# The last of the 24 sets of four weight-block sums, on VectorE in place of GpSimd

## The chip, the cores and the metric

The kernel runs on one core of one Trainium2 chip. Its time is the device time of one launch in microseconds (us); what counts is the median of several runs. The core has five engines with queues of their own: TensorE (PE in the rows), VectorE (DVE), ScalarE (ACT), GpSimd (POOL) and SyncE (SP), which here starts nearly all DMA transfers. Each queue is worked in its order, so an instruction that waits holds up everything behind it on the same engine.

## The reference

Attention over a sliding window of 64 tokens (4 batches, 8 heads, 576 tokens, 64 numbers a head), then two layers of the same form on 2304 tokens:

```
x = attention(q, k, v)                      # 2304 x 512
h = x @ w_in1;  g = h - tanh(h);            x = g @ w_out1      # 512 -> 2048 -> 512
h = x @ w_in2;  g = h * sigmoid(1.702 * h); x = g @ w_out2      # 512 -> 2048 -> 512
```

The four weight matrices arrive as 64-bit floats; the kernel makes 32-bit ones of them by bit operations on the chip.

## The kernel before, in words

**Precision.** Every operand of a large product is split into a high part (`hi`, `gh`, written by ScalarE) and the rest (`lo`, `gl`, a subtraction on VectorE), and `three` (line 783) takes three matmuls for one: high by high, high by low, low by high. So each step on TensorE needs a high part from ScalarE and then a low part from VectorE.

**Seven products for eight.** Layer 1's output product for its last two blocks of 512 tokens, and layer 2 for two units of 1024 tokens, are multiplied by Winograd's form of Strassen's method: seven block products P1 to P7, with sums and differences of blocks on both sides. On the weight side each of the 16 weight slabs, taken in pairs, gives four sums S1 to S4 (`wd_sums`, lines 394 to 400): S1 = A21 + A22, S2 = S1 - A11, S3 = A11 - A21, S4 = A12 - S2, each on 128 x 256 numbers. There are three matrices to prepare (m = 0 is layer 2's w_in, m = 1 its w_out, m = 2 layer 1's w_out) and eight pairs j of each, 24 sets in all, all on GpSimd. For m = 0 (`plan_wd`, lines 463 to 487) a pair of slabs is loaded into `raw`, ScalarE and VectorE convert it into two `cw` tiles (`conv_abs`, `conv_mant`, `conv_low`, `conv_sign`), the sums are written over the `raw` tile, and four stores by SyncE (line 433) put the two `cw` tiles and the two halves of `raw` into a DRAM tensor `wd0` to `wd7`; layer 2 reads it later (line 517). The last set made is (j, m) = (7, 0).

**The stage around the change.** While the last weights are prepared, TensorE ends layer 1's hidden products (`psh`) and begins layer 1's output products for the last two blocks (`ob`): seven products of eight steps, 56 steps, a step being six matmuls (`o_prod`, line 1064). A step's operand is a tile `ug`; for P6, P7 and P4 VectorE first forms it by a subtraction (`u_sub`, line 1040), then ScalarE writes `gh` (line 1049) and VectorE `gl` (line 1053), through three buffers of each. The weights of four steps come by one 1 MB load (`load_w1`, line 1029), 14 loads in all into three buffers: load number n can start when the steps on load n-3 are done. In the same stretch SyncE starts loads for layer 2's first unit (`xt`, line 957, and `x2b`, line 961, which VectorE adds to `xt` at line 965); an `x2b` takes one of four small buffers that its addition frees. After the 56 steps comes layer 2's first block of 256 tokens (`psh` and `acc`), and then the two units.

**What sets the order.** The class `Plan` plays the whole program through once, with an estimated length for each task and a priority from its due time; the order in which it comes to the tasks is then fixed, engine by engine. So a task's engine and estimated length can move other tasks in the order, also on other engines.

Of the kernel before, what the change touches and what calls it, by code (L numbers as in the profile page):

```python
# [24 lines left out]
class Plan:  # L25
# [11 lines left out]
    def add(self, engs, fn, prio, after=(), acq=(), rel=(), size=0, behind=None):  # L37


        t = dict(engs=engs, fn=fn, prio=prio, acq=acq, rel=rel, size=size, n=len(self.tasks), outs=[], next=[], left=0, at=None, own={})  # L40
        for a in after:
            if a is not None:
                a["outs"].append(t)
                t["left"] += 1
        if behind is not None:
            behind["next"].append(t)
            t["left"] += 1
        self.tasks.append(t)
        return t
# [126 lines left out]
def attn_moe2_kernel(  # L176
# [20 lines left out]
    nc = tc.nc  # L197
# [3 lines left out]
    _, NG, NP, _ = q.shape  # L201
# [14 lines left out]
    NJ = KF // 2  # L216
# [33 lines left out]
    add = plan.add  # L250
# [44 lines left out]
    def first(*key):  # L295
        return min(due["h", s] for s in steps if s[0][: len(key)] == key)
# [89 lines left out]
    def pair_of(j, m, i):  # L386
        layer = 1 if m == 2 else 2
        if i < 2:
            return bits[layer, 2 * j + i, m].bitcast(F32)
        return raw[layer, 2 * j, m].bitcast(F32).rearrange("p a b -> p (a b)")[:, (i - 2) * NB : (i - 1) * NB]  # L390

    PAIRS = (((A11, A12), (A21, A22), (S1, S2), (S3, S4)), ((A11, A21), (A12, A22), (S1, S2), (S3, S4)), ((A11, A21), (A12, A22), (S1, S2), (S3, S4)))

    def wd_sums(j, m):
        x = {}
        for i in range(4):
            p = pair_of(j, m, i)
            x[PAIRS[m][i][0]], x[PAIRS[m][i][1]] = p[:, :HB], p[:, HB:]
        for o, a, b, op in ((S1, A21, A22, ALU.add), (S2, S1, A11, ALU.subtract), (S3, A11, A21, ALU.subtract), (S4, A12, S2, ALU.subtract)):
            nc.gpsimd.tensor_tensor(out=x[o], in0=x[a], in1=x[b], op=op)  # L400

    def wd_hi(j, m, i):
        o = stage[j, i, 0] = st.tile([P, NB], F32R, tag="s", name="wds")
        nc.scalar.activation(o, pair_of(j, m, i), AF.Copy)
# [16 lines left out]
    def rebuild(j, i):  # L421
        if i == 0:
            raw[1, 2 * j, 2] = cv.tile([P, NB, 2], U32, tag="raw", name="raw")
        x = bits[1, 2 * j + i, 2] = st.tile([P, NB], F32, tag="cw", name="cw", bufs=K["cw"])
        hi, lo = halves((1, 2 * j + i, 1))
        nc.vector.tensor_tensor(out=x, in0=hi.bitcast(F32), in1=lo.bitcast(F32), op=ALU.add)
# [11 lines left out]
    def plan_s(j, d, near, last):  # L438
        c = [converted[1, 2 * j + i, 1] for i in range(2)]
        a = [add({"DVE": 0.62}, lambda _: rebuild(j, 0), d, c + near + last, acq=("raw", "cw", "cw"))]  # L440
        a.append(add({"DVE": 0.62}, lambda _: rebuild(j, 1), d + 1, a))
        sums = add({"POOL": 2.8}, lambda _: wd_sums(j, 2), d + 3, a)
        add({"none": 0.0}, lambda _: None, d, [sums], rel=[("cw", a[0]), ("cw", a[0])])
        sts, lows = [], []
        for i in (2, 3):
            h = add({"ACT": 0.54}, lambda _, i=i: wd_hi(j, 2, i), d + 2 * i, [sums], acq=("s", "wds"))
            lo = add({"DVE": 0.62}, lambda _, i=i: wd_lo(j, 2, i), d + 2 * i, [h])
            for b, w in enumerate((h, lo)):
                sts.append(add({"SP": 0.6}, lambda _, i=i, b=b: wd_store(j, 2, i, b), d + 2 * i, [w], size=P * NB * 4))
            add({"none": 0.0}, lambda _: None, d, [sts[-2], lo], rel=[("s", h), ("wds", h)])  # L450
            lows.append(sts[-1])
        add({"none": 0.0}, lambda _: None, d, lows, rel=[("raw", a[0])])
        wd_done[2, j] = sts
        for i in range(2):
            a_done.setdefault(2 * j + i, []).append(a[i])
        return [sums]
# [6 lines left out]
    def plan_wd(j, m, d, after):  # L463
        signs, ls, cs = [], [], []
        both = add({"SP": 1.2}, lambda _: [load_w((2, 2 * j + i, m)) for i in (1, 0)], d - 5, after, acq=("raw", "raw"), size=2 * P * NB * 8)
        for i in range(2):
            key = (2, 2 * j + 1 - i, m)

            def go(e, fn, t, *a, key=key, **kw):
                return add({e: t}, lambda _: fn(key), d + 3 * i, *a, **kw)  # L470

            l = both
            c = absol = go("ACT", conv_abs, 0.55, [l] + cs, acq=() if i else ("cw", "cw"))
            for fn, x in ((conv_mant, 0.34), (conv_low, 0.6)):
                c = go("DVE", fn, x, [c])
            signs.append(go("DVE", conv_sign, 0.6, [c], rel=[] if i else [("raw", l)]))
            ls.append(l)
            cs.append(absol)
        sums = add({"POOL": 2.8}, lambda _: wd_sums(j, m), d + 6, signs)
        los, sts = [], []  # L480
        if m == 0:
            for i in range(4):
                sts.append(add({"SP": 0.6}, lambda _, i=i: wd_store(j, 0, i), d + 6 + 2 * i, signs[1 - i :][:1] if i < 2 else [sums], size=P * NB * 4))
            wd_done[m, j] = sts
            add({"none": 0.0}, lambda _: None, d, sts[:2] + [sums], rel=[("cw", cs[0]), ("cw", cs[0])])
            add({"none": 0.0}, lambda _: None, d, sts[2:], rel=[("raw", ls[0])])
            return both
        for i in range(4):
            h = add({"ACT": 0.54}, lambda _, i=i: wd_hi(j, 1, i), d + 6 + 2 * i, signs[1 - i :][:1] if i < 2 else [sums], acq=("s", "wds") + (("s", "wds") if i < 2 else ()))
            los.append(add({"DVE": 0.62}, lambda _, i=i: wd_lo(j, 1, i), d + 6 + 2 * i, [h]))  # L490
            for b, w in enumerate((h, los[-1])):
                sts.append(add({"SP": 0.6}, lambda _, i=i, b=b: wd_store(j, 1, i, b), d + 6 + 2 * i, [w], rel=[("s", h), ("wds", h)] if b and i < 2 else [], size=P * NB * 4))
            add({"none": 0.0}, lambda _: None, d, sts[-2:-1] + los[-1:], rel=[("s", h), ("wds", h)])
        wd_done[m, j] = sts
        add({"none": 0.0}, lambda _: None, d, los[:2] + [sums], rel=[("cw", cs[0]), ("cw", cs[0])])
        add({"none": 0.0}, lambda _: None, d, [sts[5], sts[7]], rel=[("raw", ls[0])])
        return both
# [631 lines left out]
    for t, m in masks.items():  # L1129
        nc.gpsimd.memset(m, 0.0)  # L1130
        for kind, r in zip(t, (slice(0, W), slice(W, P))):
# [5 lines left out]
            for base, cm, step, op in conds:  # L1137
                nc.gpsimd.affine_select(
                    out=m[r], in_=m[r], pattern=[[step, P]], base=base,
# [8 lines left out]
    for i in range(NEARLY):  # L1148
        a = 2 * i
# [14 lines left out]
    for i in range(8):  # L1164
        z = turns[0 if i < 2 else 1 if i < 4 else 2]
        d = first(*z) - K["ahead"][i]
# [3 lines left out]
    for bi in range(2, NB1):  # L1170
        t0, n = blocks[1][bi]
        d = first(1, bi)
# [4 lines left out]
    for f in range(KF):  # L1177
        for i in range(2):
            d = due["hp"[i], next(s for s in steps if s[1] == f)]
# [278 lines left out]
    for what, s, *rest in seq:  # L1458
        if what == "O":
            if (0, 0) not in wd_done:  # L1460
                last = None
                for n in range(2 * NJ):
                    d = K["wd"][0] + K["wd"][1] * n
# [156 lines left out]
    for o in order:  # L1620
        d = due[o]
# [50 lines left out]
```

## Time and profile before

| | |
|---|---|
| median of 3 runs | 856.62 us (855.27 to 856.74) |
| profiled execution | 854.67 us |
| its span, first to last instruction | 852.9 us |
| mean granted TensorE clock | 0.992 |
| TensorE, VectorE, ScalarE, GpSimd busy | 822.5, 679.1, 469.8, 213.9 us |
| DMA, mean over the span | 218 GB/s |

The profile is of one execution. Times in its rows are us from the span's start. A busy time counts the engine's own instructions; a granted clock of 1.00 is the full one (2.4 GHz), 0.50 the lower level (1.2 GHz). A row of waits says which engine and line waited for which other, how long in all, how many times, and how long at most. In a row of the order in time, the bracket at the end is the idle time before the instruction and what ended it.

### The profile page before, as it was taken

To read this page: it belongs to the slowest core of one execution; us is meant where nothing else is said; L and a number is where in the kernel's file an instruction comes from. 1 tells how busy PE (TensorE), PEld (TensorE's weight loads), DVE (VectorE), ACT (ScalarE), POOL (GpSimd) and SP (SyncE) were. 2 spreads that over 40 slices of the span, in tenths; PEclk is the share of its full clock that TensorE was granted. 3 is DMA by queue.
4 is the path that set the end of the run, shared out by engine and by line. 5 is a ranking of instruction groups with operands and counts; after the bars stand their busy time and mean duration, and the time that the engine had idled before them with its cause. 6 is when DMAs were issued, how large, how long until landed. Compare 5 with 4: busy or idle time off the path is not lost.

```text
span 852.9 us, 15375 instructions
## 1 busy us (share of the span) xinstructions
PE 822.5 (96%) x5639; PEld 715.5 (84%) x5639; DVE 679.1 (80%) x1085; ACT 469.8 (55%) x1040; POOL 213.9 (25%) x211
## 2 busy tenths in 40 slices
PE   7898999999999999999859999999999999999998
PEld 5787888888899988887748888888899998889998
DVE  6999998879899878757939885577899867778954
ACT  7887566457677656334416654344545544444443
POOL 3110001531422213253910000366500006662000
PEclk9999999999999999999969999999999999999999
DMA  9785977788897976696367998321666742226572
GB/s 329 269 283 169 277 247 263 265 283 269 272 287 268 295 243 207 224 296 209 119 219 242 324 336 278 112 87 38 215 230 219 246 161 87 80 73 246 178 225 71
DMA packets 115163, 186.34 MB, mean 218 GB/s; under 512 B 7440, under 2 KB 81168, under 8 KB 115088
## 3 DMA queue, kind: packets, MB, share of 16 engines
q1 hardware_dynamic: 114656, 184.84, 65.5%
q8 instruction: 44, 0.72, 0.4%
q10 hardware_dynamic: 432, 0.52, 0.2%
q14 instruction: 31, 0.25, 0.1%
HBM read 131.86 MB, written 53.48 MB: 217 GB/s over the span
## 4 chain that ended last, share of the span: by engine, by line
PE 77%; DVE 9%; DMA 4%; POOL 3%; ACT 3%; issue 2%; SPq 1%; DVEq 0%; ACTq 0%; POOLq 0%
PE ob L783 23%; PE psh L783 22%; PE m L783 17%; PE acc L783 12%; POOL raw L400 3%; PE psa L701 1%; PE psa L718 1%; DMA x2b<-xs 1%; PE psa L645 1%; DMA wo<-wdo 1%; DVE gl L1053 1%; ACT s L677 1%; DVE cw L337 1%; DVE s L694 1%; DMA w<-wdo 1%
## 5 line engine op out<-in xcount | busy, mean ns | idle before, releaser
L783 PE MATMUL psh<-xh,w 128*128 128x512 f32 (+1 forms) x672 | 194.7, 362 | 0.0
L1049 ACT ACTIVATE gh<-ug 128x512 fp32r<-128x512 f32 x168 | 105.2, 629 | 110.3 <-PE ob L783 96.5
L783 PE MATMUL ob<-ws,gh 128*128 128x256 f32 x896 | 162.0, 283 | 0.0
L1053 DVE TENSOR_TENSOR gl<-ug,gh 128x512 fp32r<-128x512 f32 x168 | 120.6, 721 | 42.8 <-ACT gh L1049 40.3
L783 PEld LDWEIGHTS ob<-ws,gh 128*128 128x128 f32 x896 | 140.0, 192 | 0.2
L783 PEld LDWEIGHTS psh<-xh,w 128*128 128x128 f32 x672 | 121.6, 189 | 20.2 <-issue 1.0
L1037 POOL TENSOR_TENSOR ug<-ug,g 128x512 f32<-128x512 f32 x48 | 68.2, 1428 | 256.2 <-ACT g L1033 255.9
L783 PE MATMUL ob<-ws,gl 128*128 128x256 f32 x448 | 126.9, 283 | 1.7 <-DVE gl L1053 1.7
L783 PE MATMUL psh<-xl,w 128*128 128x512 f32 (+1 forms) x336 | 120.9, 360 | 1.6 <-DVE xl L738 1.6
L400 POOL TENSOR_TENSOR raw<-cw 128x256 f32<-128x256 f32 x48 | 59.3, 1236 | 240.8 <-DVE cw L343 84.6
L783 PE MATMUL acc<-gh,w 128*128 128x512 f32 (+1 forms) x416 | 113.4, 344 | 0.0
L783 PE MATMUL m<-xu,ws 128*128 128x512 f32 x384 | 92.3, 389 | 0.0
L783 PEld LDWEIGHTS ob<-ws,gl 128*128 128x128 f32 x448 | 86.0, 192 | 2.0 <-DVE gl L1053 1.9
L783 PEld LDWEIGHTS m<-xu,ws 128*128 128x128 f32 x384 | 71.9, 188 | 14.9
L783 PE MATMUL ob<-gh,w 128*128 128x512 f32 x224 | 71.6, 398 | 12.4 <-DMA w<-wdo 12.3
L783 PEld LDWEIGHTS acc<-gh,w 128*128 128x128 f32 x416 | 73.6, 189 | 9.9 <-issue 0.9
L1011 DVE TENSOR_TENSOR ug<-ug,m 128x512 f32<-128x512 f32 x80 | 54.8, 685 | 31.2 <-PE m L783 30.0
L783 PEld LDWEIGHTS psh<-xl,w 128*128 128x128 f32 x336 | 63.5, 189 | 11.1 <-DVE xl L738 2.2
L783 PE MATMUL acc<-gl,w 128*128 128x512 f32 (+1 forms) x208 | 70.8, 340 | 0.0
L526 DVE TENSOR_TENSOR ws<-wr,ws 128x1024 fp32r<-128x1024 f32 (+1 forms) x40 | 53.6, 1343 | 10.3 <-ACT ws L521 10.0
L783 PEld LDWEIGHTS ob<-gh,w 128*128 128x128 f32 x224 | 43.0, 192 | 22.2 <-issue 12.7
L521 ACT ACTIVATE ws<-wr 128x1024 fp32r<-128x1024 f32 (+1 forms) x40 | 38.7, 969 | 41.4 <-PE m L783 33.0
(119 smaller groups left out, 1471.0 us busy)
## 6 DMA issues: line engine op xcount, KB each, us to landing
ws<-wdo SPq DMA_DIRECT2D x28, 1024.0 KB, 5.3
raw<-in_w_in SPq DMA_DIRECT2D x32, 512.0 KB, 5.5
raw<-in_w_out SPq DMA_DIRECT2D x32, 512.0 KB, 4.7
w<-wdo SPq DMA_DIRECT2D x14, 1024.0 KB, 6.5
wdo<-wds SPq DMA_DIRECT2D x48, 256.0 KB, 3.2
wr<-wd SPq DMA_DIRECT2D x24, 512.0 KB, 6.3
wdo<-w SPq DMA_DIRECT2D x32, 256.0 KB, 4.8
wdo<-raw SPq DMA_DIRECT2D x32, 256.0 KB, 3.4
```

What stands on the lines that cost most here:

```text
L337: nc.vector.scalar_tensor_tensor(out=bits[key], in0=raw[key][:, :, 0], scalar=29, in1=bits[key], op0=ALU.logical_shift_right, op1=ALU.bitw ...
L400: nc.gpsimd.tensor_tensor(out=x[o], in0=x[a], in1=x[b], op=op)
L521: nc.scalar.activation(new_ws(key)[:, 0, : x.shape[1]], x, AF.Copy)
L526: nc.vector.tensor_tensor(out=t[:, 1], in0=x, in1=t[:, 0].bitcast(F32), op=ALU.subtract)
L645: nc.tensor.matmul(ps[h][part(j, h), p, :], lhsT=qt[j][r, p, :], rhs=kt[j][r, :, p, :], start=not on_pe, stop=not on_pe or p == NP - 1,)
L677: nc.scalar.activation(s[:, h, p, :], x[:, p, :], AF.Exp, bias=nm[:, h, p : p + 1], scale=scale, accum_out=sm[:, h, p : p + 1],)
L694: nc.vector.tensor_tensor(out=s[:, h], in0=s[:, h], in1=sm[:, h].unsqueeze(2).to_broadcast([P, NP, P]), op=ALU.mult)
L783: nc.tensor.matmul(ps, lhsT=a, rhs=b, start=first and i == 0, stop=last and i == 2, skip_group_check=onto)
L1011: nc.vector.tensor_tensor(out=u_val(u, j, o), in0=u_val(u, j, a), in1=mb[u, j, n], op=ALU.add)
L1037: eng.tensor_tensor(out=u_val(u, j, o), in0=u_sum(u, j, o), in1=ut[u, j, o, "g"], op=ALU.mult)
L1049: nc.scalar.activation(gh, u_val(u, j, PROD[n][1]), AF.Copy)
L1053: nc.vector.tensor_tensor(out=gl, in0=u_val(u, j, PROD[n][1]), in1=gh.bitcast(F32), op=ALU.subtract)
```

## The change

The set (7, 0) is planned for VectorE with an estimated length of 1.6 us, where all sets were planned for GpSimd with 2.8 us; `wd_sums` takes the engine as an argument. The other 23 sets stay on GpSimd.

```
-    def wd_sums(j, m):
+    def wd_sums(j, m, eng):
...
         for o, a, b, op in ((S1, A21, A22, ALU.add), (S2, S1, A11, ALU.subtract), (S3, A11, A21, ALU.subtract), (S4, A12, S2, ALU.subtract)):
-            nc.gpsimd.tensor_tensor(out=x[o], in0=x[a], in1=x[b], op=op)
+            (nc.vector if eng == "DVE" else nc.gpsimd).tensor_tensor(out=x[o], in0=x[a], in1=x[b], op=op)
...
-        sums = add({"POOL": 2.8}, lambda _: wd_sums(j, 2), d + 3, a)
+        sums = add({"POOL": 2.8}, lambda g: wd_sums(j, 2, g), d + 3, a)
...
-        sums = add({"POOL": 2.8}, lambda _: wd_sums(j, m), d + 6, signs)
+        sums = add({"DVE": 1.6} if (j, m) == (NJ - 1, 0) else {"POOL": 2.8}, lambda g: wd_sums(j, m, g), d + 6, signs)
```

On GpSimd the four instructions of the set go and nothing else moves; TensorE's order is the same. On VectorE the set comes in behind the second `conv_sign` (line 343) of the pair. There, in the kernel before, stands (`gl_4930` belongs to the ninth of the 56 steps, `raw_4828` and the two `cw` are the pair's tiles, `xt` and `x2b` the input of layer 2's first unit):

```order
L343 SCALAR_TENSOR_TENSOR cw_4871<-raw_4828,cw_4871 128x512
L1053 TENSOR_TENSOR gl_4930<-ug_3864,gh_4929 128x512
L965 TENSOR_TENSOR xt_4846<-xt_4846,x2b_4883 128x256
L1040 TENSOR_TENSOR ug_3864<-ug_3864 128x512
L1053 TENSOR_TENSOR gl_4948<-ug_3993,gh_4947 128x512
L1040 TENSOR_TENSOR ug_3864<-ug_3864 128x512
```

and in the changed one:

```order
L343 SCALAR_TENSOR_TENSOR cw_4871<-raw_4828,cw_4871 128x512
L1053 TENSOR_TENSOR gl_4930<-ug_3864,gh_4929 128x512
L400 TENSOR_TENSOR raw_4828<-cw_4872 128x256
L400 TENSOR_TENSOR raw_4828<-raw_4828,cw_4871 128x256
L400 TENSOR_TENSOR raw_4828<-cw_4871,cw_4872 128x256
L400 TENSOR_TENSOR raw_4828<-cw_4871,raw_4828 128x256
L1053 TENSOR_TENSOR gl_4944<-ug_3993,gh_4943 128x512
L1053 TENSOR_TENSOR gl_4961<-ug_4070,gh_4960 128x512
L1040 TENSOR_TENSOR ug_3864<-ug_3864 128x512
```

The four sums take the place of an addition to `xt` and a subtraction; that addition now stands 28 low parts further on, behind the one of step 37, and the subtractions run about one place later than before.

On SyncE the stores of this set stand between the fifth and the sixth weight load. Before (`w1_4966` is the fifth load, `w1_5022` the sixth, `wd7` the DRAM tensor of the set):

```order
L1029 DMA w1_4966<-wdo2_740 128x2x1024
L433 DMA wd7_4917<-raw_4828 128x512
L433 DMA wd7_4917<-raw_4828 128x2x256
L961 DMA x2b_4992<-xs1_10_2997 128x256
L961 DMA x2b_5009<-xs0_4_2561 128x256
L1029 DMA w1_5022<-wdo2_740 128x2x1024
```

Changed (`w1_4963` is the fifth load, `w1_5014` the sixth):

```order
L1029 DMA w1_4963<-wdo2_740 128x2x1024
L433 DMA wd7_4917<-raw_4828 128x512
L433 DMA wd7_4917<-raw_4828 128x2x256
L961 DMA x2b_4989<-xs1_10_2997 128x256
L1029 DMA w1_5014<-wdo2_740 128x2x1024
```

One `x2b` load fewer stands ahead of the sixth weight load, and the stores stay where they were. That `x2b` load comes later in the changed kernel, between the eleventh weight load (`w1_5251`) and the twelfth (`w1_5308`):

```order
L1029 DMA w1_5251<-wdo2_740 128x2x1024
L1112 DMA xs4_0_5258<-ou_4966 128x512 x2
L517 DMA wr_5289<-wd0_3807 128x1024
L961 DMA x2b_5296<-xs0_4_2561 128x256
L1029 DMA w1_5308<-wdo2_740 128x2x1024
L961 DMA x2b_5315<-xs1_10_2997 128x256
```

It takes the buffer of `x2b_4883`, so it stands behind the moved addition on VectorE.

## Rows read from the trace of the kernel before

**Rows 1.** The page: busy time, share of the span, instructions

```profile
PE 822.5 (96%) x5639; PEld 715.5 (84%) x5639; DVE 679.1 (80%) x1085; ACT 469.8 (55%) x1040; POOL 213.9 (25%) x211
```

**Rows 2.** Chain that ended last, 385 to 480 us: start, length, what

```profile
406.59 20.07 POOL raw L400
...
430.30 5.85 DMA w<-wdo
...
436.29 39.05 PE ob L783 x162
```

**Rows 3.** Waits, 396 to 440 us: us in all, times, longest

```profile
PE ob L783 <- DMA w<-wdo: 12.3, 1, 12.3
```

**Rows 4.** Waits of SyncE's queue, 396 to 440 us

```profile
SPq L433 <- POOL raw L400: 19.8, 2, 18.9
```

**Rows 5.** Line 400, whole run: ns min/median/max, first and last start

```profile
L400 POOL TENSOR_TENSOR raw<-cw x48: 722/742/20055, 142.5 to 427.4; 128x256 f32<-128x256 f32 x48
```

**Rows 6.** SyncE in order of time: start, length, line, transfer

```profile
407.98 0.53 SPq L1029 DMA_DIRECT2D w<-wdo  x1
427.47 1.73 SPq L433 DMA_DIRECT2D wd<-raw  x2
...
430.30 19.73 SPq L1029 DMA_DIRECT2D w<-wdo  x5
```

**Rows 7.** TensorE in order of time, within the 56 steps

```profile
409.08 0.39 PE L783 MATMUL ob<-gl,w 128*128 128x512 f32 x1
...
409.76 0.39 PE L783 MATMUL ob<-gl,w 128*128 128x512 f32 x1
...
412.71 0.61 PE L783 MATMUL ob<-gh,w 128*128 128x512 f32 x2
...
423.59 0.39 PE L783 MATMUL ob<-gh,w 128*128 128x512 f32 x1
436.29 0.77 PE L783 MATMUL ob<-gh,w 128*128 128x512 f32 x1 [12.31 <-DMA w<-wdo]
...
440.92 0.63 PE L783 MATMUL ob<-gh,w 128*128 128x512 f32 x2
```

**Rows 8.** Stretches: length, busy us (instructions) by engine, TensorE clock, DMA share, GB/s

```profile
436.30:440.70 4.40, 4.40 (x11) 3.44 (x12) 0.81 (x2) 0.63 (x1) 0.00 (x0) 0.50 0.88 359
440.70:480.00 39.30, 39.23 (x173) 32.19 (x172) 36.88 (x61) 24.11 (x39) 0.00 (x0) 1.00 0.73 245
480.00:520.00 40.00, 39.77 (x245) 35.42 (x244) 31.11 (x56) 22.82 (x43) 0.00 (x0) 1.00 1.01 334
```

**Rows 9.** VectorE in order of time, around the set and behind it

```profile
400.91 0.43 DVE L334 TENSOR_SCALAR cw<-cw 128x512 uint32<-128x512 uint32 x1 [0.88 <-ACT cw L331]
401.37 0.69 DVE L337 SCALAR_TENSOR_TENSOR cw<-raw,cw 128x512 uint32<-128x512 uint32 x1
...
406.37 0.69 DVE L1053 TENSOR_TENSOR gl<-ug,gh 128x512 fp32r<-128x512 f32 x1
406.98 0.42 DVE L965 TENSOR_TENSOR xt<-xt,x2b 128x256 f32<-128x256 f32 x1
407.31 0.68 DVE L1040 TENSOR_TENSOR ug<-ug 128x512 f32<-128x512 f32 x1
407.91 0.68 DVE L1053 TENSOR_TENSOR gl<-ug,gh 128x512 fp32r<-128x512 f32 x1
...
425.37 0.69 DVE L1040 TENSOR_TENSOR ug<-ug 128x512 f32<-128x512 f32 x1
439.88 0.69 DVE L1053 TENSOR_TENSOR gl<-ug,gh 128x512 fp32r<-128x512 f32 x1 [13.82 <-ACT gh L1049]
...
457.65 0.75 DVE L965 TENSOR_TENSOR xt<-xt,x2b 128x256 f32<-128x256 f32 x2
```

**Rows 10.** Line 1029, the 14 weight loads: from issue to landing

```profile
DMA to landing us min/median/max: 5.1/6.5/9.9
```

**Rows 11.** Tile x2b, its 16 loads: from issue to landing

```profile
DMA to landing us min/median/max: 2.3/4.6/10.2
```

## The prediction

> **What bounds the kernel now.** I read the page first: TensorE is busy for 96% of the span and VectorE for 80% [rows 1], so time is won where TensorE stands or runs slowly, and only there. Next the chain of work that ended last: nearly all of it is matmuls, with one foreign piece in the middle, a GpSimd sum of line 400 that lasts 20.07 us, then a weight load, then matmuls again [rows 2]. The waits of that stretch say what it did to TensorE: one wait of 12.3 us for a weight load [rows 3]. SyncE's waits say why that load was late: SyncE stood at line 433, the stores of the sums, for GpSimd, 18.9 us in one piece [rows 4]. In the order of time, the fifth weight load was started at 407.98, the store at 427.47, and the sixth load only at 430.30 [rows 6]. So the path is: sums on GpSimd, store, sixth weight load behind it on SyncE, TensorE.
>
> Why was the sum slow? A sum of this line takes 742 ns in the median; this one took 20055 ns [rows 5]. It started at 406.59 [rows 2], inside a stretch in which VectorE has no gap: no idle time stands in front of its instructions up to the one at 425.37, and the sum ended at 406.59 + 20.07 = 426.66, once VectorE had nothing left to do and stood for 13.82 us [rows 9]. I read that as GpSimd being kept out while VectorE works without a gap on operands that both lie in SBUF.
>
> **The change part by part.**
>
> *The stall that goes.* TensorE's last matmul before the wait starts at 423.59 and the next one would have started one matmul later. The pace is read between the two low-part matmuls of step 10, 409.08 and 409.76: 0.68 us for three, 0.227 us each. So the next was due at 423.82 and started at 436.29 [rows 7]: 12.47 us.
>
> *The slow clock behind it.* After the wait the granted clock is 0.50 for the next 4.4 us, the lower level (1.2 GHz), and 1.00 again from there [rows 8]. From 436.29 to 440.92 [rows 7] eleven matmuls start, 4.63 us where 11 x 0.227 = 2.49 us would do: 2.14 us. Without the wait this goes too. Together 14.6 us.
>
> *What is late next.* The sixth load needs the buffer of the third, which step 12's last matmul frees: it starts at 412.71 and takes 0.39 us [rows 7], so about 413.1, and some 0.3 us later with the delay below. With the sums done by 409 the stores and one `x2b` load are out before that, so the sixth load starts at some 413.4. It lands 6.5 us later in the median, 9.9 at most [rows 10], so at 419.9 to 423.3, and is wanted for step 21 at 423.82 plus the same delay. Even the slowest landing of the 14 just fits. The loads after it have the same room: a buffer is free eight steps before its new weights are wanted, 8 x 1.36 = 10.9 us. I take no wait here; if the landing were 2 us slower than the slowest row, each would cost 2 us.
>
> *What the sums cost on VectorE.* The trace has no sum of line 400 on VectorE. The nearest row from below is the addition of the same shape and type at line 965: two of them in a row take 0.75 us, one 0.42, so 0.33 us from one start to the next [rows 9]: 4 x 0.33 = 1.3 us. From above: S2 needs S1 and S4 needs S2, and where an instruction waits for the result just before it, line 337 behind line 334, the starts are 0.46 us apart [rows 9]: 4 x 0.46 = 1.8 us. The sums start where the addition stands now, at 406.98. Step 10's low part then starts at 408.3 to 408.8 in place of 407.91 (the addition and one subtraction, 0.33 + 0.60, have moved behind it) and ends 0.69 later, at 409.0 to 409.5. TensorE takes it at 409.08 [rows 7, 9]. So TensorE waits between 0 and 0.5 us; I take 0.3, near the upper end, as three of the four depend on an instruction close before. The bound below nothing is excluded: the low part cannot come sooner than the one it already had without waiting.
>
> *What VectorE has to carry later.* From there its list is the old one, about 1.2 us late (1.5 for the sums, less the 0.33 of an addition), and TensorE no longer gives it 13.82 us to catch up. Per step VectorE needs a low part and at most about one more instruction of 0.60, 1.2 us of TensorE's 1.36, so it gains some 0.16 us a step. Behind the stall, with TensorE at full clock, it was busy for 36.88 of 39.3 us [rows 8] and TensorE lost nothing to speak of (39.23 busy). The work that the change moves from before the stall to behind it is one addition and about one subtraction, 0.33 + 0.60 = 0.9 us, against 39.3 - 36.88 = 2.4 us spare. It fits, with 1.5 us left; I charge 0.2 us for a low part that comes just late, bounds 0 and 2.
>
> *What VectorE's additions wait for.* The moved addition, now behind step 37's low part, and two `x2b` loads behind it make VectorE wait for a transfer in the middle of its list. The load of `x2b_5296` starts as soon as that addition is done; it is used about 4 us further on in VectorE's list, and lands after 4.6 us in the median, 10.2 at most [rows 11]. At the median VectorE stands for about 0.6 us, which its lead over TensorE covers; at the most it stands for some 6 us, of which I put the lead at 2: 4 us on TensorE. I take 0.1, as nothing else then fills the queues (0.73 of DMA's time is used in that stretch, [rows 8]).
>
> *What GpSimd loses* is four instructions with nothing behind them for the rest of the stage (its busy time from 436.30 to 480 is zero, [rows 8]): nothing.
>
> *Sum.* 14.6 - 0.3 - 0.2 - 0.1 = 14.0 us. The profiled execution took 854.67 us, 1.8 more than its span of 852.9: 854.67 - 14.0 = 840.7. The median of the runs, 856.62, stands 1.95 above the profiled one; with the same offset, 842.6 us.
>
> **The rivals.**
>
> *A. VectorE or its loads become the bound.* For it: it is 94% busy behind the stall (36.88 of 39.3, [rows 8]) and starts later into this list. Against it: the spare 2.4 us and the buffers' lead. Price: the 2 us and 4 us above in place of 0.2 and 0.1, at most 5.7 more; the middle of it 3 us, so 845.6.
>
> *B. The gain is given back in the next stage.* From 480 to 520 DMA is busy all the time, at 334 GB/s, where it was at 0.73 and 245 GB/s before [rows 8]. If layer 2's loads come at a pace that only DMA sets, TensorE waits there for what it won. Against it: these loads start behind matmuls, `ug` steps and buffers, so they start 14 us earlier too, and the stretch ahead has a quarter of DMA's time free. Moving all bytes of 440.7 to 480 (39.3 us x 245 GB/s = 9.6 MB) takes 29 us at 334 GB/s, so the stretch can be made 10 us denser in itself. Price: half of the gain, 7 us, so 849.6.
>
> *C. It makes no difference.* The sum's 20 us could be only its recorded span, with the sixth load waiting for a buffer. Against it: the buffer was free at 413.1, and SyncE's own wait names the sums to 427.47 [rows 4, 6, 7]. Then 856.6. In another form: if GpSimd got a turn after each VectorE instruction, its first sum would wait 0.69 us at most [rows 9], the set would be done by about 411, and SyncE would have no such wait to lose; the gain would again be zero. The rows speak against it: 20.07 us [rows 2], through all of VectorE's instructions from 406.98 to 425.37, without a turn. The Trainium skill (SBUF — State Buffer, "Who interferes with whom") states the rule behind this form: a VectorE instruction with two SBUF inputs and a GpSimd instruction that reads SBUF contend for one shared port pair, an exclusive lock held for the whole instruction, by whichever issues first. It says nothing of a loser that stays out over many instructions, which the trace shows here.
>
> *D. Slower: SyncE is now held by VectorE.* The load of `x2b_5296` stands ahead of the twelfth weight load, and waits for an addition that has moved 28 low parts down VectorE's list. The twelfth load's buffer is free when step 36 ends and its weights are wanted at step 45: 10.9 us, less 6.5 for landing [rows 10], leaves 4.4. Each us by which VectorE reaches that addition more than 4.4 us after step 36 is a us for TensorE, and a wait of such length brought 2.14 us of slow clock. It decides for slower from 4.4 + (14.3 - 2.1) = 16.6 us late. Such a lag needs another block like the one of 20.05 us: 20.05 - 4.4 + 2.1 = 17.8, so 842.6 + 17.8 = 860.4. Against it: VectorE waits only for three buffers' worth of steps and for TensorE itself, and no GpSimd instruction is left in this stretch to contend with.
>
> **How the numbers follow.** Forecast, 842.6: 0.82, with a range of its own from 841 to 844.5. A: 0.09. B: 0.04. C: 0.03. D: 0.02. A change under 0.2% (1.7 us) cannot be told from none, so faster means below 854.9: the forecast, A and B, 0.95; same is C, 0.03; slower is D, 0.02. The range goes from 840.8 (no costs, and 1 us of the offset between profile and runs less) to 846.5, which takes in the forecast and most of A.
>
> **What would show it.** Right: no sum near 20 us is left on line 400; the store of the two `raw` halves starts within 2 us of the fifth weight load, and the sixth load starts near 413; TensorE has no wait over 1 us between 395 and 470, and the clock stays at 1.00 there; its first matmul of step 21 starts at about 424; layer 2's units start some 14 us earlier. The four sums take 1.3 to 1.8 us on VectorE, with a wait of up to 0.5 us on TensorE just behind. Wrong: a new wait of TensorE for a low part around steps 38 to 46 (A), for `wr`, `wo` or `xt` between 470 and 510 (B), or for the twelfth weight load (D); or the same wait as before with another name in front (C).

## The result, and the profile after

| | before | after |
|---|---|---|
| median | 856.61 us (4 runs, 855.27 to 856.74) | 842.81 us (4 runs, 839.71 to 843.66) |
| profiled execution, its span | 854.67, 852.9 us | 842.52, 840.7 us |
| first matmul of the 56 steps, from there to the span's end | 395.75, 457.15 us | 398.21, 442.49 us |

The ratio is 0.9836, 95% interval 0.9809 to 0.9863: faster, by 13.8 us. Five more rounds of the same kernel (e0 below) gave 840.75 us. The two spans differ by only 12.2 us, because the profiled execution after came to the stage 2.46 us late, 2.0 of it from its first 40 us (TensorE's 401st matmul starts at 37.47 in place of 35.43), and runs of either order show such a start (35.57 in e1, 37.72 in e4); from the stage's first matmul on the difference is 457.15 - 442.49 = 14.66 us.

Page, busy time, against [rows 1]: TensorE's time is the same, in a shorter span.

```profile
PE 822.9 (98%) x5639; PEld 715.7 (85%) x5639; DVE 679.2 (81%) x1089; ACT 469.0 (56%) x1040; POOL 192.2 (23%) x207
```

TensorE's waits, 395 to 480 us, against [rows 3] (us in all, times, longest), then SyncE's at the stores of the sums, against [rows 4]:

```profile
PE ob L783 <- DVE gl L1053: 0.5, 2, 0.3
PE ob L783 <- ACT gh L1049: 0.2, 1, 0.2
```

```profile
SPq L433 <- POOL raw L400: 1.4, 1, 1.4
```

The wait for a weight load is gone. The 1.4 us in the second view belong to an earlier set, since this one is no longer on GpSimd; its stores start 0.6 us behind the fifth weight load, and the sixth starts once its buffer is free. SyncE in order of time, against [rows 6]:

```profile
410.54 0.53 SPq L1029 DMA_DIRECT2D w<-wdo  x1
411.17 1.02 SPq L433 DMA_DIRECT2D wd<-raw  x2
...
415.92 27.72 SPq L1029 DMA_DIRECT2D w<-wdo  x6
```

Less the 2.46 us, that is 413.46, where the kernel before started it at 430.30. VectorE around the four sums, against [rows 9], and the slowest sum left on GpSimd, 1192 ns, where [rows 5] had 20055:

```profile
408.93 0.69 DVE L1053 TENSOR_TENSOR gl<-ug,gh 128x512 fp32r<-128x512 f32 x1
409.53 0.42 DVE L400 TENSOR_TENSOR raw<-cw 128x256 f32<-128x256 f32 x1
409.98 0.42 DVE L400 TENSOR_TENSOR raw<-raw,cw 128x256 f32<-128x256 f32 x1
410.33 0.42 DVE L400 TENSOR_TENSOR raw<-cw 128x256 f32<-128x256 f32 x1
410.66 0.42 DVE L400 TENSOR_TENSOR raw<-cw,raw 128x256 f32<-128x256 f32 x1
411.00 1.29 DVE L1053 TENSOR_TENSOR gl<-ug,gh 128x512 fp32r<-128x512 f32 x2
```

```profile
L400 POOL TENSOR_TENSOR raw<-cw x46: 727/740/1192, 145.1 to 394.2; 128x256 f32<-128x256 f32 x46
```

Stretches, against [rows 8] (length, busy us of TensorE, its weight loads, VectorE, ScalarE, GpSimd, with instructions; clock, DMA share, GB/s):

```profile
408.40:424.00 15.60, 15.60 (x70) 12.66 (x69) 15.57 (x29) 7.83 (x13) 0.00 (x0) 1.00 0.87 271
424.00:470.00 46.00, 45.71 (x202) 37.54 (x201) 45.14 (x75) 28.05 (x45) 0.00 (x0) 1.00 0.77 262
470.00:510.00 40.00, 40.00 (x250) 36.06 (x250) 29.79 (x55) 21.80 (x43) 0.00 (x0) 1.00 1.03 352
```

No stretch has a clock of 0.50. From 424 to 470 VectorE is busy for 45.14 of 46.00 us and TensorE still loses only 0.29; from 470 to 510 DMA is busy throughout and TensorE loses nothing.

### The profile page after: what moved, and what is told of

Its sections match the earlier page's. It is cut to its first block, busy times and chain, and to the rows that moved or that the text cites. A ratio compares the mean times of both kernels' runs of the same rounds, so it can differ in the third digit from the quotient of the medians.

```text
span 840.7 us, 15367 instructions
## 1 busy us (share of the span) xinstructions
PE 822.9 (98%) x5639; PEld 715.7 (85%) x5639; DVE 679.2 (81%) x1089; ACT 469.0 (56%) x1040; POOL 192.2 (23%) x207
## 4 chain that ended last, share of the span: by engine, by line
PE 66%; DVE 4%; ACT 2%; issue 1%; DMA 1%; SPq 0%; POOL 0%; DVEq 0%; ACTq 0%
PE ob L783 26%; PE m L783 18%; PE psh L783 15%; PE acc L783 5%; PE psa L718 1%; PE psa L701 1%; PE psa L645 1%; ACT wds L404 0%; ACT s L677 0%; DVE gl L818 0%; DMA x2b<-xs 0%; DVE gl L1053 0%; DVE s L660 0%; DVE raw L409 0%; DVE nm L663 0%
## 5 line engine op out<-in xcount | busy, mean ns | idle before, releaser
L400 POOL TENSOR_TENSOR raw<-cw 128x256 f32<-128x256 f32 x46 | 38.8, 843 | 231.6 <-DMA wdo<-w 78.6
L783 PE MATMUL ob<-gh,w 128*128 128x512 f32 x224 | 69.9, 390 | 0.2 <-ACT gh L1049 0.2
L526 DVE TENSOR_TENSOR ws<-wr,ws 128x1024 fp32r<-128x1024 f32 (+1 forms) x40 | 53.6, 1343 | 10.1 <-ACT ws L521 9.8
L331 ACT ACTIVATE cw<-raw 128x512 f32<-128x512 f32 x64 | 42.9, 679 | 24.3 <-DMA raw<-in_w_in 9.2
```

What stands on the lines that cost most here:

```text
L331: nc.scalar.activation(bits[key].bitcast(F32), raw[key].bitcast(F32)[:, :, 1], AF.Abs, scale=2.0**-112)
L400: (nc.vector if eng == "DVE" else nc.gpsimd).tensor_tensor(out=x[o], in0=x[a], in1=x[b], op=op)
L526: nc.vector.tensor_tensor(out=t[:, 1], in0=x, in1=t[:, 0].bitcast(F32), op=ALU.subtract)
L783: nc.tensor.matmul(ps, lhsT=a, rhs=b, start=first and i == 0, stop=last and i == 2, skip_group_check=onto)
```

## Experiments

The change does two things: it puts the sums on another engine, and by the planned length it moves VectorE's list (the addition of line 965 and an in-place subtraction of line 1040 no longer stand between the sums' place and step 10's low part). Theory 1 is the prediction's: GpSimd is kept out as long as VectorE works without a gap, so the engine is what matters. Theory 2: the order is. Times are medians, ratios are to the kernel before on the same chip (its medians there 854.99 to 856.5 us). The last column runs from the first matmul of the 56 steps to the end of the profiled span, which leaves the start-up out.

| kernel | median, us | ratio, 95% interval | first sum, us | stage to end, us |
|---|---|---|---|---|
| before | 856.61 | | 20.07 | 457.15 |
| e0, the change | 840.75 | 0.982 (0.9803 to 0.9836) | 0.42, VectorE | 442.07 |
| e1, order alone | 840.88 | 0.9825 (0.9806 to 0.9843) | 1.06 | 442.68 |
| e2, engine alone | 841.35 | 0.9831 (0.9814 to 0.9848) | 0.42, VectorE | 443.41 |
| e3, stores late | 846.92 | 0.9894 (0.9878 to 0.991) | 20.06 | 447.56 |
| e4, addition later | 843.5 | 0.985 (0.9821 to 0.9879) | 1.07 | 444.52 |
| e5, addition back | 840.79 | 0.9827 (0.98 to 0.9855) | 2.00 | 442.76 |
| e6, gap ahead | 845.69 | 0.9897 (0.9873 to 0.9922) | 1.06 | 445.86 |

**e0: the change again.** No edit.

> The changed kernel once more, beside the others of this set. Every theory: 842.8 us, within 840 to 844, some 13.8 less than the kernel before.

TensorE's only wait in the stage was 0.3 us for a low part, and the time 840.75 us. The result holds.

**e1: the order alone.** The order of the changed kernel, the sums on GpSimd:

```
-lambda g: wd_sums(j, m, g), d + 6, signs)
+lambda g: wd_sums(j, m, "POOL"), d + 6, signs)
```

> The order of the changed kernel on every engine (the set is planned for VectorE), but the four sums are issued to GpSimd. Theory 1 (GpSimd is kept out by VectorE's unbroken work, and SyncE stands at the store): the first sum lasts some 20 us again, TensorE waits some 12 us for the sixth weight load, 856 us (854 to 858). Theory 2 (the gain is from the order: one x2b load fewer ahead of the sixth weight load, and the additions to xt later): 843 us, with no wait on TensorE.

It is as fast as the change, and theory 1 falls in the form in which I had stated it: GpSimd's four sums took turns with VectorE, whose instructions grew from 0.69 to about 1.2 us meanwhile. The start of a sum's row is taken here as the moment when GpSimd asks. GpSimd, then VectorE: the low part under which GpSimd asked, and the next one:

```profile
406.18 1.06 POOL L400 TENSOR_TENSOR raw<-cw 128x256 f32<-128x256 f32 x1 [9.66 <-DMA wd<-cw]
407.32 1.07 POOL L400 TENSOR_TENSOR raw<-raw,cw 128x256 f32<-128x256 f32 x1
408.36 1.19 POOL L400 TENSOR_TENSOR raw<-cw 128x256 f32<-128x256 f32 x1
409.50 1.19 POOL L400 TENSOR_TENSOR raw<-cw,raw 128x256 f32<-128x256 f32 x1
```

```profile
405.96 0.69 DVE L1053 TENSOR_TENSOR gl<-ug,gh 128x512 fp32r<-128x512 f32 x1
...
406.60 1.19 DVE L1053 TENSOR_TENSOR gl<-ug,gh 128x512 fp32r<-128x512 f32 x1
```

Without a wait an instruction of 128x512 follows 0.60 us after the one before it [rows 9], which is called VectorE's pace below; here the second came 0.64 later, a gap of 0.04 us, since its high part ended only at 406.58.

**e2: the engine alone.** The order of the kernel before, the four sums on VectorE ahead of the addition of line 965 and the subtraction:

```
-lambda _: wd_sums(j, m), d + 6, signs)
+lambda g: wd_sums(j, m, "DVE" if (j, m) == (NJ - 1, 0) else g), d + 6, signs)
```

> The order of the kernel before on SyncE, ScalarE and TensorE (the set is planned as for GpSimd), but the four sums are issued to VectorE, ahead of the addition and the subtraction that the change moves behind them. Theory 1: 842.8 us (841 to 845); the wait of TensorE behind the sums is up to 1.2 us instead of 0.2, as the next low part is 0.9 us later. Theory 2: near 856 us, since the order is that of before.

Theory 2 falls too: without the new order the time is 841.35 us, and TensorE waits 0.9 us at most for a low part. Either half of the change is enough by itself. The question is what the lock-out hangs on, the 20 us in which GpSimd got no turn.

**e3: the stall's way through SyncE.** The kernel before, with the two stores of the set's `raw` halves moved in SyncE's list behind the last weight load:

```
...
+        got = [t for t in got if not any(t is x for x in late_stores)]
+        spot = next(i for i, t in enumerate(got) if t is w1_loads[13]) + 1
+        got[spot:spot] = late_stores
```

> The kernel before, sums on GpSimd, but SyncE's two stores of this set stand behind the 14th weight load. Theory 1: the first sum still lasts 20 us or more (until VectorE's list first has a pause, 432 to 460), but nobody waits for it: no wait of TensorE for the sixth load, 842.5 us (840 to 845), as fast as the change without any sum on VectorE. Theory 3 (the time is lost to the slow sums themselves, through GpSimd or through what they hold of VectorE, not through the store in SyncE's queue): near 856 us.

The first sum was kept out as before, and TensorE did not wait for a weight load: the wait does come through SyncE's store, as the prediction's chain had it. The time is still 1.9 us above theory 1's range: of the 15.1 us from stage to end that e0 gains, 9.6 came. TensorE lost 1.0 us at a low part while the sums took their turns, and the rest is the price of the stores' new place. There SyncE waited 7.9 us for their landing ahead of layer 2's loads (line 517, here 520); ScalarE stood 5.34 us for such a load ahead of its next high part; TensorE waited 2.0 us for that part and 0.8 for the low part behind it, and then had a stretch at a clock of 0.50, some 1.7 us more. GpSimd's first sum, then VectorE near its end (line 1056 is the low part, 1043 the subtraction), then SyncE's wait, ScalarE's, and the slow stretch (as in [rows 8]):

```profile
405.92 20.06 POOL L400 TENSOR_TENSOR raw<-cw 128x256 f32<-128x256 f32 x1 [9.38 <-DVE cw L343]
```

```profile
424.69 0.70 DVE L1043 TENSOR_TENSOR ug<-ug 128x512 f32<-128x512 f32 x1
425.38 1.15 DVE L1056 TENSOR_TENSOR gl<-ug,gh 128x512 fp32r<-128x512 f32 x1
```

```profile
SPq L520 <- DMA wd<-raw: 8.5, 2, 7.9
```

```profile
471.68 1.06 ACT L524 ACTIVATE ws<-wr 128x1024 fp32r<-128x1024 f32 x1 [5.34 <-DMA wr<-wd]
```

```profile
475.90:478.90 3.00, 3.00 (x9) 2.33 (x9) 1.28 (x2) 2.35 (x3) 0.00 (x0) 0.50 1.07 350
```

The start at 425.38 is 0.69 us after the one before it, 0.09 more than VectorE's pace. GpSimd's first sum ended 0.60 us after that late start, so it got in at this gap; the other three sums then took turns (1.07, 1.18, 1.18 us).

**m1: what keeps GpSimd out.** A small program of its own; the list with two SBUF inputs is

```
nc.vector.tensor_tensor(out=d[i], in0=x, in1=y, op=ALU.add)       # i = 0 to 23
nc.gpsimd.tensor_tensor(out=p[n], in0=d[3][:, :256], in1=b[:, 256:], op=ALU.add)   # n = 0 to 3
```

> Not the reference: it leaves the whole computation out and measures four additions of 128x256 on GpSimd (two SBUF inputs), started after the fourth of 24 VectorE instructions of 128x512, in seven forms of the VectorE stream: none, two SBUF inputs, one input in PSUM, one SBUF input (scalar), scalar with two SBUF inputs, two SBUF inputs with each instruction using the result before it, two SBUF inputs with a pause for ScalarE at every sixth. Theory 1 (kept out by back-to-back instructions with two SBUF inputs): without a stream 0.74 us a sum; two SBUF inputs, both forms: the first sum lasts to the end of the stream, 20 x 0.60 = 12 us; one input in PSUM: 0.74 us; chained: the pauses of 0.1 us between instructions let GpSimd in, so 0.8 to 2 us a sum; with a pause every sixth: the first sum lasts to the first pause, about 1 us on, and the others 0.74 to 4. A rival (the lock goes to whoever issued first, instruction by instruction): 0.7 to 1.4 us a sum in every form, none near 12 us.

(Tiles lie in one of two memories, SBUF or PSUM; TensorE's results come into PSUM, and most of the kernel's tiles lie in SBUF.) Four sums alone took 2.76 us, beside additions with two SBUF inputs 4.42, with one of them in PSUM 2.77, beside `tensor_scalar` 3.36, and beside the other three forms 3.98 to 4.55. Nowhere was GpSimd kept out. Two SBUF inputs do cost turns, but a turn was always to be had, so theory 1 lacked a condition. Between these lists and the kernel's stood the short addition of line 965 right behind GpSimd's request, the waits that the kernel's instructions carry, and the gaps.

**e4 and e5: the short addition.** In e4, the kernel before, the addition changes places with the subtraction behind it; in e5, which is e1, it is put back behind the low part under which GpSimd asks. Both by moving one task in the planned order:

```
...
+        moved = got.pop(old)
+        after = [i for i, t in enumerate(got) if i > sign and t["on"] == "DVE"]
+        got.insert(after[1] + 1, moved)      # e5: after[0] + 1
```

> The kernel before, all sums on GpSimd, with a single edit: the addition of 128x256 (line 965) that VectorE does right behind the gl under which GpSimd's first sum begins comes one place later, behind the in-place subtraction (line 1040) that followed it. Theory 'short addition': it is this instruction of 0.33 us, the first that VectorE starts after GpSimd has asked, that lets GpSimd miss its turn; then the first sum lasts about 1.1 us, the four sums under 5 us, no weight-load wait stays, and the time is about 842 us (840.5 to 844). Theory 'no gap': GpSimd only enters where VectorE's next instruction comes late; here the in-place subtraction is ready at once, so that the first sum lasts about 20 us again and the time stays at 856 us. Theory 'chance of the phase': either, but then the addition has nothing to do with it.

> The kernel e1 (order of the changed kernel, all sums on GpSimd; its first sum lasted 1.06 us and its time was 840.9 us), with the addition of 128x256 (line 965) put back right behind the gl under which GpSimd's first sum begins, as in the kernel before. Theories 'short addition' and 'no gap' agree here: the sum is kept out again for some 15 to 20 us, until VectorE has a gap, and the time is about 853 to 857 us, with the wait for the sixth weight load back. If the sums last 1.0 to 1.2 us each again and the time is about 841 us, then it is neither of the two, and what VectorE does later (in-place subtractions between all gl) is what keeps GpSimd out.

e4 gave the numbers of "short addition", e5 refuted it: there the addition stands where it stood, and the sum took 2.00 us, not 15 to 20. VectorE behind the request at 409.81 in e5:

```profile
409.59 0.68 DVE L1053 TENSOR_TENSOR gl<-ug,gh 128x512 fp32r<-128x512 f32 x1
410.19 0.42 DVE L965 TENSOR_TENSOR xt<-xt,x2b 128x256 f32<-128x256 f32 x1
410.53 0.68 DVE L1053 TENSOR_TENSOR gl<-ug,gh 128x512 fp32r<-128x512 f32 x1
411.55 0.81 DVE L1053 TENSOR_TENSOR gl<-ug,gh 128x512 fp32r<-128x512 f32 x1 [0.34 <-ACT gh L1049]
```

Two instructions passed GpSimd by, and it got in where VectorE waited for ScalarE; I had not seen that this gap would come so early. In e4 the subtraction, now first, was not ready at once: it started 0.72 us after the low part, 0.12 late.

```profile
408.39 0.68 DVE L1053 TENSOR_TENSOR gl<-ug,gh 128x512 fp32r<-128x512 f32 x1
409.11 1.12 DVE L1040 TENSOR_TENSOR ug<-ug 128x512 f32<-128x512 f32 x1
```

So in every run of the kernel so far GpSimd got in at the first gap of VectorE after it had asked, however short: 0.04 us in e1. e4 is still 1.8 us behind e5 from stage to end: TensorE's waits for low parts are 1.3 us there against 0.5, and it waits 0.8 us for VectorE (line 810) in layer 2's first block, where e5 has no wait.

**m2 and m3: gaps or waits.** Two more programs of additions; their lists, a letter for each (in m2 p and q are additions of 512 and 256 columns, e of 128, h line 965's kind, g a low part, s in place):

```
m2: "p" * 20, "pq" + "p" * 18, "ph" + "p" * 18, "pe" + "p" * 18, "p" + "q" * 24, "g" * 16,
    "gh" + "g" * 15, "gs" * 10, "gh" + "sg" * 9, "pq" + "sg" * 9, "s" * 20
m3: "n" * 20, "w" * 20, "n" + "w" * 19, ..., "wwwwww" + "n" * 14, "wwwwww" + "x" + "w" * 13
```

> Not the kernel: a small program that leaves the whole computation out and runs eleven lists of additions on VectorE, each with four sums of 128x256 on GpSimd that are asked for as the second instruction of the list starts. Lists, in order: 128x512 throughout; the same with one 128x256 as the third instruction; the same with that one in place behind a DMA; with one 128x128; 128x256 throughout; subtractions that wait for ScalarE; those with a 128x256 in place as the second; those in turn with in-place subtractions; those with both, which is what stands in the kernel before; the same without the DMA; in-place subtractions throughout. Theory 'short addition': the first sum lasts 0.7 to 1.4 us in the lists 1, 6, 8 and 11 and over 9 us in 2, 3, 7, 9 and 10. Theory 'no gap': over 9 us in all lists in which VectorE never waits. Theory 'mixed list' (in-place subtractions and waits that are already met keep it out): over 9 us in 8 to 10 alone. If it is 0.7 to 1.4 us in all, the lists lack what matters.

"No gap" held: in six lists the first sum lasted over 9 us, and in the five where it lasted about 1 us an addition wrote a tile that the one just before it had written or read, a real wait. The second list, where GpSimd got in at once, and the third, where it was kept out (VectorE's instruction under which it asked, its first sum, VectorE's next; a row with x2 holds the next one too):

```profile
31.64 1.55 DVE L53 TENSOR_TENSOR d<-t,b 128x512 f32<-128x512 f32 x2
31.87 1.03 POOL L100 TENSOR_TENSOR p<-d,b 128x256 f32<-128x256 f32 x1 [6.22 <-DVE d L53]
32.36 1.96 DVE L53 TENSOR_TENSOR d<-t,b 128x256 f32<-128x256 f32 x2
...
51.67 0.68 DVE L53 TENSOR_TENSOR d<-t,b 128x512 f32<-128x512 f32 x1
51.90 12.21 POOL L100 TENSOR_TENSOR p<-d,b 128x256 f32<-128x256 f32 x1 [15.87 <-DVE d L53]
52.27 0.42 DVE L53 TENSOR_TENSOR xt<-xt,x2b 128x256 f32<-128x256 f32 x1
```

From 31.64 to 32.36 are 0.72 us, 0.12 more than the pace; from 51.67 to 52.27 it is the pace. But the first list, nothing but additions, was kept out, and m1's second, which looked the same, was not.

> Not the kernel: it leaves the whole computation out and runs eleven lists of 20 additions of 128x512 on VectorE, all alike but for what they wait for, each with four sums of 128x256 on GpSimd that are asked for as the first addition of the list begins. An addition waits (w) on an event of VectorE that is long past, or on nothing (n), or for the addition right before it (x, a real wait of some hundredths of a us). Lists: all n; all w; n then w; w then n; n, w, then n; w and n in turn; six w, one n, w; six w, two n, w; six w, three n, w; six w, n to the end; six w, x, w. Theory 'waits': GpSimd keeps out while VectorE's instructions carry a wait, met or not, and gets its turn where one that waits on nothing follows another such, or where a wait is real: the first sum lasts 1.0 to 1.4 us in lists 1 and 4 and 5 (there one or two instructions later, up to 2.5), about 4 to 6 us in lists 8 to 11, over 9 us in 2, 3, 6 and 7. Theory 'gap alone': over 9 us in lists 1 to 10, about 4.5 us in 11. Theory 'chance' (which clock edge comes first): no relation to the letters.

Theory "waits" fell: whatever an addition carries, ten lists took 14.5 us, and only the one with a real wait, as its seventh instruction, 7.44. The first row and the last of GpSimd's eleven, and VectorE at the wait of the last list, 0.72 us from start to start:

```profile
16.70 14.58 POOL L56 TENSOR_TENSOR p<-r,b 128x256 f32<-128x256 f32 x4 [16.26 <-DVE r L44]
...
296.30 7.44 POOL L56 TENSOR_TENSOR p<-r,b 128x256 f32<-128x256 f32 x4 [13.44 <-DVE r L44]
```

```profile
299.08 0.68 DVE L52 TENSOR_TENSOR late<-t,b 128x512 f32<-128x512 f32 x1
299.80 1.09 DVE L52 TENSOR_TENSOR old<-late,b 128x512 f32<-128x512 f32 x1
```

**m4 and m5: m1's exception.** m3 had 20 additions ahead of the one that GpSimd waits for, m1 three.

```
m4: for i in range(ahead): add(...)      # ahead 3 or 20, then the producer, then 20 more
m5: ahead 1 to 8 with 512 columns; 4, 6, 8, 10, 12, 16 with 256
```

> Not the kernel: it leaves the whole computation out. The additions of m1, whose second list let GpSimd in at once though VectorE showed no gap, against those of m3, whose first list, the same additions without a wait, kept it out to the end. Ten lists of 20 additions of 128x512, with four sums of 128x256 on GpSimd asked for as each list begins; they differ in how many additions stand ahead of the one that the sums wait for (3 as in m1, 20 as in m3), in whether that one writes its tile a second time (m1) or not (m3), and in the tiles that it and the list read (a or t; the sums read its result and b). Lists 1 and 2 are m1's. Theory 'gap alone' with something of m1 that makes a gap too small to see: the lists with m1's feature take 4.4 us for the four sums (the first 1.0), the others 14.5 us, and the feature shows by which lists these are: writing twice gives 1, 2, 4, 5, 6; three ahead gives 1, 2, 3, 5, 6, 8; reading a in the list gives 1 to 4, 6, 9, 10. Theory 'chance': lists 1 and 2, which are the same, may differ, and no feature fits.

Lists 1, 2, 5, 6 and 8 took 4.4 us, the others 14.5. That is none of the three sets exactly: of the lists with three ahead only the third is missing, and it is the only one of them that did not begin with a real wait: its first addition starts 0.21 us after the copy of 128x256 ahead of it, those of lists 2, 5, 6 and 8 start 0.31 or 0.32 us after it. So what counts, it seemed, is how long VectorE has already worked without a gap when GpSimd asks.

> Not the kernel: it leaves the whole computation out. Fourteen lists; in each VectorE has a real wait (for the tile t), then does 1, 2, 3, 4, 5, 6, 7 or 8 additions of 128x512 (0.60 us each), or 4, 6, 8, 10, 12 or 16 of 128x256 (0.33 us each), then the one that GpSimd's four sums wait for, then 20 more without a gap. Theory 'since the last gap': in m4 GpSimd got its turn where it asked up to 3.25 us (the fifth addition) after VectorE's last wait and was kept out where it asked 13 us after, in m2 5.6 us (the tenth), in the kernel before some 4 us (the seventh); so the first lists of 128x512 take 4.4 us for the four sums, from 5 or 6 ahead on they take 14.5. The lists of 128x256 tell time from count: by time, GpSimd gets in up to 8 or 10 ahead and is kept out at 12 and 16; by count, it is kept out from 6 ahead on. Theory 'chance' or another feature of the head: no clean border.

A clean border in the lists of 128x512. The fourth and fifth list, VectorE's additions ahead (from the last wait on) and GpSimd's four sums:

```profile
54.36 2.50 DVE L32 TENSOR_TENSOR more<-t,b 128x512 f32<-128x512 f32 x4
...
72.24 3.10 DVE L32 TENSOR_TENSOR more<-t,b 128x512 f32<-128x512 f32 x5
```

```profile
57.60 4.43 POOL L42 TENSOR_TENSOR p<-d,b 128x256 f32<-128x256 f32 x4 [13.46 <-DVE d L32]
76.09 14.52 POOL L42 TENSOR_TENSOR p<-d,b 128x256 f32<-128x256 f32 x4 [14.06 <-DVE d L32]
```

Asked under the sixth instruction since the wait, 3.24 us after it, GpSimd got its turn; asked under the seventh, 3.85 us after, it was kept out to the end of the list. m1's second list fits: GpSimd asked at 11.70, also under the sixth, 3.25 us after the wait. So do the lists of m4 that got in: they asked under the sixth, list 8 under the fifth (the expectation above has the latest of them, at 3.25 us, under the fifth). In the kernel before it also asked under the seventh (402.75 is the first, 406.37 [rows 9] the seventh, at 0.60 each), 3.84 us after VectorE's last gap, which the trace of before has here, 0.09 us ahead of 402.75:

```profile
402.23 0.43 DVE L334 TENSOR_SCALAR cw<-cw 128x512 uint32<-128x512 uint32 x1 [0.17 <-ACT cw L331]
402.75 0.69 DVE L1053 TENSOR_TENSOR gl<-ug,gh 128x512 fp32r<-128x512 f32 x1
403.36 0.68 DVE L343 SCALAR_TENSOR_TENSOR cw<-raw,cw 128x512 uint32<-128x512 uint32 x1
```

Counted from the wait that the profile marks, ahead of 402.23, it was the eighth; either count lies past the border.

The lists of 128x256 were all kept out, the first of them 2.32 us after the wait and under the eighth instruction (two copies, which I had not counted, follow the wait): that speaks for a count of instructions and against a time. As no list of 128x256 here let GpSimd in, the other side of the border is not shown at that length.

**e6: the condition in the kernel.** The kernel before, order and engine unchanged, with a gap made ahead of the set's last conversion (line 343):

```
...
+            if t is marks[NJ - 1, 0]:
+                z = [gp.tile([P, 1], F32, tag=f"z{n}", name="z", bufs=1) for n in range(2)]
+                nc.vector.memset(z[0], 0.0)
+                nc.vector.tensor_copy(z[1], z[0])
             t["fn"](t["on"])
```

> The kernel before, all sums on GpSimd and its order unchanged, but for two tiny instructions on VectorE ahead of the last sign insertion of the set (line 343), about 1 us before GpSimd asks: 128x1 is set to zero and copied, and the copy waits for the first, a gap of some hundredths of a us. All that follows the request stands as before: gl, the addition of 128x256, the in-place subtractions, without a gap. Theory 'since the last gap': GpSimd, which asked 4 us after VectorE's last gap and was kept out 20 us, now asks 1 us after it; the first sum lasts 0.9 to 1.3 us, no weight-load wait stays, and the time is 840.5 to 844 us, ratio 0.982 to 0.987. Theory 'gap after the request alone': the first sum lasts 19 to 20 us again and the time is 855 to 857 us.

The first sum took 1.06 us although VectorE's list behind the request is that of the kernel before, without a gap: GpSimd asked under the third instruction since the wait of the copy. VectorE, and GpSimd:

```profile
406.65 0.06 DVE L1640 MEMSET z<- 128x1 f32 x1
406.76 0.15 DVE L1641 COPY z<-z 128x1 f32<-128x1 f32 x1
406.83 0.68 DVE L343 SCALAR_TENSOR_TENSOR cw<-raw,cw 128x512 uint32<-128x512 uint32 x1
407.43 0.68 DVE L1053 TENSOR_TENSOR gl<-ug,gh 128x512 fp32r<-128x512 f32 x1
408.03 0.96 DVE L965 TENSOR_TENSOR xt<-xt,x2b 128x256 f32<-128x256 f32 x1
408.92 1.22 DVE L1040 TENSOR_TENSOR ug<-ug 128x512 f32<-128x512 f32 x1
```

```profile
407.64 1.06 POOL L400 TENSOR_TENSOR raw<-cw 128x256 f32<-128x256 f32 x1 [9.14 <-DMA wd<-cw]
```

No weight-load wait stayed. The time is 1.7 us above the range that I gave: step 10's low part now stood behind two instructions that took turns with GpSimd, and TensorE waited 1.2 us for it, 1.8 in all in the stage. e6 is 3.8 us longer than e0 from stage to end. Matmul by matmul, 0.7 us of that came ahead of the set, 1.8 in steps 10 to 14, and 1.3 in small steps behind; the first and the last I have not traced to a cause.

## Why the prediction was right, and where it was not

*Time and path.* 842.6 us was predicted, 842.81 measured. The path (sum, store on SyncE, sixth load, TensorE) is shown by e3, which removes the wait without touching the sum. The lower end of the range was summed wrongly: no costs and 1 us less of the offset give 842.6 - 0.6 - 1.0 = 841.0, not 840.8.

*The gross gain, 14.6 us.* Measured, with costs, 14.66. The sixth load was put at 413.4 and came at 413.46 (less the late start); no load was late behind it, with landings of 5.1 to 10.1 us against 5.1 to 9.9 before [rows 10].

*The costs, 0.6 us.* The sums took 1.47 us on VectorE (409.53 to 411.00), inside 1.3 to 1.8; TensorE waited at most 0.3 us, as taken. VectorE did not wait for an `x2b` between 424 and 480, where I had charged 0.1. The rest of the 0.6 cannot be told from nothing: two profiles of the changed kernel end 442.49 and 442.07 us after the stage begins. VectorE is tighter than I reckoned, 0.86 us spare in 46 where I had 2.4 in 39.3, and it was still enough: rival A was nearer than it looked. B is out (no loss from 470 to 510 at a DMA share of 1.03), D too: TensorE has no wait for the twelfth load.

*The step that was too wide.* "I read that as GpSimd being kept out while VectorE works without a gap on operands that both lie in SBUF." For this set it is true, and as a rule it is not: in e6, m1, m4 and m5 GpSimd got turns beside a VectorE without a gap. What the trace of before could not show is that a second condition counts: VectorE had already begun its seventh instruction or later since its last wait when GpSimd asked. Rival C's other form, a turn after each VectorE instruction, which I held to be refuted by the rows, is what happens when GpSimd asks earlier than that. The Trainium skill (SBUF — State Buffer, "Who interferes with whom") has the shared port pair locked for an instruction by whichever issues first; the turns agree with it (1.06 to 1.19 us a sum, VectorE's instructions 1.2), the 20.06 us of e3 go beyond it.

*Luck in the reason.* The sums had not to leave GpSimd: e1 is as fast with them there. The change removed the lock-out twice over. A gap of 0.04 us at the right place would have done, and that the kernel before had none there is an accident of its order: three other orders (e1, e4, e5) had one.

## What to carry to other kernels

A GpSimd instruction many times longer than its median, beside a VectorE list without idle time, may have been passed by, as here; look at what waits for it, and at how many instructions VectorE had done since its last wait. Work that something in order stands behind does not belong on GpSimd beside a VectorE that works without a gap on two SBUF inputs, unless a short real wait of VectorE lies within the few instructions ahead of it. And where a change moves both an engine and an order, run each alone before believing either.

## What the runs showed of the hardware

- GpSimd sums of 128x256 (SBUF to SBUF) beside VectorE instructions with two SBUF inputs: when GpSimd asked under the third to sixth instruction since VectorE's last wait (e6, m1, m4, m5) it got in at the next boundary, and the two took turns from then on. Under the seventh or later it was passed by until VectorE next had a gap: 20.07 us in the kernel, 10 to 12.5 us, to the end of the list, in m2 and m3. Gaps of 0.04 us (e1), 0.09 (e3) and 0.12 (e4, m2) let it in. Whether the border is a count of instructions was tried at one other length only, and from one side; why there is one stays open.
- Beside VectorE instructions that read one input from PSUM the four sums took 2.77 us, as alone (2.76).
